# Seven block products for both matrix products of tiles 3 to 8, in 12 groups of 28 units

## The chip, the cores and the metric

The kernel runs on one core of a Trainium2 chip. The metric is the device time of one execution in microseconds (us). Engines are named as in the profile: PE (TensorE, matrix products), PEld (its weight loads), DVE (VectorE), ACT (ScalarE), POOL (GpSimd), SP (SyncE, which here issues all DMAs). SBUF is the on-chip working memory, PSUM the eight banks that TensorE accumulates in.

## The reference

Windowed attention over 8 batches of 8 heads, 576 positions of 64 values, then a two-layer network on the 4608 tokens:

```python
scores = scale * np.matmul(q, k.transpose(0, 1, 3, 2))
scores = np.where(masks[None, :, :, :], scores, -1000000000.0)
attn = softmax(scores)                 # 4 heads: the last 32 positions; 4 heads: every 4th of the last 128
x = np.matmul(attn, v)                 # brought to (4608, 512)
h = x @ w_in                           # 512 -> 2048
g = np.maximum(h, 0.0) + alpha * np.minimum(h, 0.0)
out = g @ w_out                        # 2048 -> 512
```

## The kernel before

**Precision.** Each fp32 operand of the two large products is split in a high and a low part of type fp32r, and a product is three passes: high x high, high x low, low x high (`PASSES`). A "high" is an ACT copy into fp32r, a "low" the subtraction of the high part from the value.

**Tokens.** They are cut in nine tiles of 512. Tiles 0 to 2 go through plain products in 48 *slices* (one tile, one of 16 blocks f of 128 hidden channels): `ffn_h` 12 matmuls, then the activation, then `ffn_y` 12 matmuls. The loop over n (L904 and L974) runs them one slice apart; in between it does attention for 20 pairs of heads (there are 32), the conversion of the weights, and from slice 24 on it writes the weight parts to DRAM (`save`, L442) and combines the four blocks of two neighbouring f of `w_in` into four more (`combine`, L458, on GpSimd, one 2 x 256-column set in 6 instructions; `combined_high`, L471, on ACT; `combined_low`, L476, on DVE and then two DMAs). There are 8 such sets.

**Paired stage** (`paired_stage`, L764). Tiles 3 to 8 are done in pairs (t = 3, 5, 7). For a pair, the product x @ w_in is seen as a product of 2 x 2 blocks: two tiles by two f on one side, two halves of the input channels on the other. Instead of eight block products seven are made, of combined weights and combined token blocks, whose sums give the four hidden blocks (numbered 11, 12, 21, 22: the first digit is the f, the second the tile). A block product is 6 matmuls of 128 x 128 by 512 columns (`product`, L563). `Four` (L584) is the object of one such set of four hidden blocks: `mm(q)` is block product q into bank A, B or C; `snap` an ACT copy of bank A in the middle of the sums; `add` a DVE addition of a bank and a snap; `negative` an ACT Relu(-x); `value` the DVE multiply-add that makes the activation; `high` and `low` the split into `gp`, which the second product reads. `phase_h` (L663) does four sets (28 block products), each set's vector work beside the products of the next; `phase_y` (L693) then does the second product plainly: for 4 output blocks c, 8 f and 2 tiles, 3 matmuls each, 192 in all, and 16 units of weights. There are two groups per pair. The vector work of the fourth set stands behind the first 12 matmuls of `phase_y`, and its hidden blocks are used last within each c.

**Attention** in the paired stage: 12 pairs of heads, hung on steps of `phase_y` (`attention_hooks`, L733): scores on PE, maxima on DVE, exponentials on ACT, divisions on DVE, transposes on PE, copies on ACT, values on PE, copies into the raw tokens on ACT and DVE. `token_parts` (L540) makes the seven token blocks of the next pair from raw tokens.

**Order.** Each engine executes its instructions in the order in which the program is written; nothing is reordered. Weights come from DRAM through a ring of 10 slots of 256 KB (`feed`, `take`, L513 to L520), one `feed` behind each use, on SP. PSUM has eight banks: a0 to a3 for the first product, y0 to y3 for the second.

## Time and profile before

| | |
|---|---|
| median of 3 runs | 919.82 us (919.0 to 921.11) |
| the profiled execution, its own time | 919.12 us |
| its span, first to last instruction | 917.3 us |
| mean granted TensorE clock | 0.978 |
| slices, about | up to 382.7 us |
| paired stage, three pairs of tiles | 382.7 to 574, to 749.7, to 913.2 us |

The profile's second part shows how the load is spread over the span (each digit is the busy share of one of 40 equal slices, in tenths; PEclk is the granted TensorE clock, in tenths).

```profile
PE   4668999979999998999999999999999999999998
DVE  6999487686766675676345746673347627503731
ACT  6776455453535444365445543554456306303610
POOL 0000000030222541000000000000000000000000
PEclk9879999999999998999999999999999999999999
```

Busy time counts how long instructions were in an engine; matmuls overlap each other, so their mean duration is longer than the distance from one to the next.

### The profile page before, as it was taken

Reading aid. Unit: us, or ns where it says so; the run is one execution under the profiler, and the core shown is the slowest. Engines: PE = TensorE matmul, PEld = TensorE weight load, DVE = VectorE, ACT = ScalarE, POOL = GpSimd, SP = SyncE. Lnnn points to the kernel's source line nnn. Section 1 sums busy time; section 2 is a strip of 40 time slices with the busy share of each in tenths; the row PEclk is TensorE's granted clock in tenths of the full one; section 3 lists DMA queues with packets and bytes.
Section 4 is the critical chain, followed back from the end, with each engine's and each line's share of the span. In section 5 each row is a group of like instructions: output and inputs, shape, how many; then the busy total and the mean of one; then the engine's idle time right before and its main releaser. Section 6 shows DMA issues by size and latency. Waiting matters only on the chain.

```text
span 917.3 us, 20648 instructions
## 1 busy us (share of the span) xinstructions
PE 869.6 (95%) x8080; PEld 714.5 (78%) x8080; DVE 549.4 (60%) x1607; ACT 428.1 (47%) x1250; POOL 48.8 (5%) x54
## 2 busy tenths in 40 slices
PE   4668999979999998999999999999999999999998
PEld 4556888868877886888778877887888888888886
DVE  6999487686766675676345746673347627503731
ACT  6776455453535444365445543554456306303610
POOL 0000000030222541000000000000000000000000
PEclk9879999999999998999999999999999999999999
DMA  9842152216798984475557656665466456435641
GB/s 334 295 138 70 47 189 93 91 53 202 253 305 268 305 277 152 145 209 163 174 176 200 172 179 192 201 173 155 150 165 182 145 161 195 137 103 157 183 132 46
DMA packets 101313, 159.83 MB, mean 174 GB/s; under 512 B 8416, under 2 KB 47456, under 8 KB 101216
## 3 DMA queue, kind: packets, MB, share of 16 engines
q1 hardware_dynamic: 101216, 158.51, 55.8%
q8 instruction: 64, 1.05, 0.5%
q14 instruction: 33, 0.27, 0.1%
HBM read 124.92 MB, written 33.55 MB: 173 GB/s over the span
## 4 chain that ended last, share of the span: by engine, by line
PE 87%; DVE 7%; ACT 2%; DMA 1%; issue 1%; SPq 1%; DVEq 0%; ACTq 0%
PE y L705 28%; PE pA L567 14%; PE h L375 14%; PE y L422 13%; PE pC L567 7%; PE pB L567 4%; PE o L266 3%; PE s L192 3%; PE t L248 2%; DMA ws<-w_in 1%; ACT w_dt.float L228 1%; DVE w_dt.float L216 1%; DVE w_dt.float32r L363 1%; DVE wa L352 0%; DMA w_dt.uint<-w_out 0%
## 5 line engine op out<-in xcount | busy, mean ns | idle before, releaser
L375 PE MATMUL h<-x,w_dt.float32r 128*128 128x512 f32 x576 | 150.7, 414 | 7.3 <-DVE nm L216 6.9
L422 PE MATMUL y<-g,w_dt.float32r 128*128 128x512 f32 x576 | 140.7, 393 | 0.0
L375 PEld LDWEIGHTS h<-x,w_dt.float32r 128*128 128x128 f32 x576 | 114.2, 201 | 33.0 <-issue 7.3
L422 PEld LDWEIGHTS y<-g,w_dt.float32r 128*128 128x128 f32 x576 | 106.6, 188 | 22.4 <-ACT ob L434 0.4
L705 PE MATMUL y<-gp,ring_w 128*128 128x512 f32 x480 | 113.7, 392 | 0.0
L705 PE MATMUL y<-gp,ring_xA 128*128 128x512 f32 x444 | 104.7, 391 | 1.0 <-issue 1.0
L705 PEld LDWEIGHTS y<-gp,ring_w 128*128 128x128 f32 x480 | 89.3, 188 | 18.6
L705 PEld LDWEIGHTS y<-gp,ring_xA 128*128 128x128 f32 x444 | 82.8, 188 | 18.4 <-issue 1.1
L228 ACT ACTIVATE pr<-pr,nm 128x64 f32<-128x64 f32 (+1 forms) x240 | 80.1, 335 | 28.7 <-DVE nm L216 28.7
L609 ACT COPY stage<-pA 128x512 f32<-128x512 f32 x72 | 42.3, 587 | 104.3 <-PE pA L567 104.3
L402 ACT CAST g<-m 128x512 fp32r<-128x512 f32 x48 | 29.8, 621 | 72.5 <-DVE m L397 66.2
L635 DVE TENSOR_TENSOR gp<-n,gp 128x512 fp32r<-128x512 f32 x96 | 63.2, 684 | 0.0
L627 DVE SCALAR_TENSOR_TENSOR n<-n,bal,stage 128x512 f32<-128x512 f32 x72 | 53.9, 749 | 13.9 <-ACT n L623 13.1
L567 PE MATMUL pA<-parts_w,ring_w 128*128 128x512 f32 x234 | 57.7, 390 | 0.0
L631 ACT CAST gp<-n 128x512 fp32r<-128x512 f32 x96 | 56.6, 615 | 1.9 <-DVE n L627 1.9
L567 PE MATMUL pA<-parts_w,ring_xA 128*128 128x512 f32 x228 | 56.2, 390 | 0.5 <-ACT raw_xB L302 0.5
L705 PE MATMUL y<-gp,ring_g 128*128 128x512 f32 x228 | 55.0, 393 | 0.0
L216 DVE CUSTOM_DVE_ANT_0 pr<-s,mask_sb 128x64 f32<-128x64 f32 (+1 forms) x288 | 45.0, 213 | 16.3 <-PE s L192 15.2
L623 ACT ACTIVATE n<-stage 128x512 f32<-128x512 f32 x72 | 45.6, 633 | 12.5 <-DVE stage L616 12.0
L567 PEld LDWEIGHTS pA<-parts_w,ring_w 128*128 128x128 f32 x234 | 43.8, 188 | 9.1
L728 DVE TENSOR_TENSOR ob<-y,py 128x512 f32<-128x512 f32 x24 | 16.4, 691 | 57.4 <-PE y L705 57.4
L567 PEld LDWEIGHTS pA<-parts_w,ring_xA 128*128 128x128 f32 x228 | 42.7, 188 | 9.5 <-ACT raw_xB L302 0.6
(104 smaller groups left out, 1213.5 us busy)
## 6 DMA issues: line engine op xcount, KB each, us to landing
ring_w<-wS SPq DMA_DIRECT2D x68, 256.0 KB, 2.8
ring_xA<-wS SPq DMA_DIRECT2D x67, 256.0 KB, 2.8
v<-vW SPq DMA_DIRECT2D x24, 576.0 KB, 3.9
ring_w<-wO SPq DMA_DIRECT2D x40, 256.0 KB, 2.8
ring_xA<-wO SPq DMA_DIRECT2D x37, 256.0 KB, 2.7
out<-ob SPq DMA_DIRECT2D x36, 256.0 KB, 3.2
ring_g<-wS SPq DMA_DIRECT2D x33, 256.0 KB, 2.8
wO<-w_dt.float32r SPq DMA_DIRECT2D x32, 256.0 KB, 5.2
```

The source lines that it names most:

```text
L216: nc.vector.tensor_tensor_reduce(out=self.pr[rows, r, :], in0=self.ps[e][rows, g, :], in1=mask_sb[rows, kind, :], scale=-SCALE, scalar=3.0 ...
L228: nc.scalar.activation(out=self.pr[rows, r, :], in_=self.pr[rows, r, :], func=AF.Exp, bias=self.nm[rows, r:r + 1], scale=-1.0, accum_out=s ...
L375: nc.tensor.matmul(ms[t, f], lhsT=weight(0, a, f)[:, c * P:(c + 1) * P], rhs=half(t, c)[:, e, :], start=(c == 0 and n == 0), stop=(c == NC ...
L402: nc.scalar.copy(out=g[:, 0, :], in_=ms[t, f])
L422: nc.tensor.matmul(ys[t][c], lhsT=weight(1, a, f)[:, c * P:(c + 1) * P], rhs=g[:, e, :], start=(first and n == 0), stop=(last and n == 2),)
L567: nc.tensor.matmul(to, lhsT=w[:, (2 * a + c) * P:(2 * a + c + 1) * P], rhs=part_of(name, e)[:, c * TT:(c + 1) * TT], start=start and c == ...
L609: nc.scalar.copy(out=self.s(n), in_=self.A)
L623: nc.scalar.activation(out=self.m[n], in_=self.at(n), func=AF.Relu, scale=-1.0)
L627: nc.vector.scalar_tensor_tensor(out=self.m[n], in0=self.m[n], scalar=bal[:, f:f + 1], in1=self.at(n), op0=ALU.mult, op1=ALU.add)
L631: nc.scalar.copy(out=self.g(n)[:, 0], in_=self.m[n])
L635: nc.vector.tensor_tensor(out=g[:, 1], in0=self.m.pop(n), in1=g[:, 0].bitcast(F32), op=ALU.subtract)
L705: nc.tensor.matmul(ys2[tt], lhsT=w[:, k * P:(k + 1) * P], rhs=g[:, e], start=j == 0 and n == 0, stop=j == GF - 1 and n == 2)
```

## The change

**Both products by seven.** The second product g @ w_out is now also seen as 2 x 2 blocks (two tiles by two output halves on one side, the two f of a set on the other) and made by seven block products. Of the four hidden blocks of a set, three (22, 12, 11) are split as before, and four combinations T1 to T4 of the blocks are formed (`sum`, DVE) and split too: seven splits a set where there were four. Their highs are ACT's; the low part of 22 is DVE's and the six others are GpSimd's.

**Groups of 28 units.** A group is now two sets (j = 0, 1), with four groups per pair of tiles, 12 in all. A unit is 6 matmuls and one slot of weights: units 0 to 13 are the first product's seven, alternately for j = 0 and 1; units 14 to 27 the second's seven, for output halves m = 0 and 1, each with 3 matmuls from either set. `Out.add` puts a finished bank into an SBUF result (ACT copy for three of them in a pair's first group, otherwise a DVE addition). The ring has 12 slots.

**Everything at fixed units.** `put(n, ...)` hangs an operation behind the matmuls of unit n, counted over the whole stage; `hidden` gives the places of a set's vector work, `attention` those of a pair of heads, which now come two per group in the first four groups of t = 3 and the first two of t = 5.

**Weights.** The four combinations of both matrices: 16 sets instead of 8, made in slices 23 to 27 and 31 to 41. The stores of f = 0 to 7 move to slices 8 to 15.

Core of the diff:

```diff
-GP = 4
-GF = 2 * GP
-NRING = 10
+GP = 2
+NGRP = NFP // GP
+FIRST = NFP // 2
+NRING = 12
+UNITS = 28
...
+    HORDER = (1, 7, 6, 4, 5, 2, 3)
+    YORDER = (1, 5, 6, 3, 7, 2, 4)
...
+        def sum(self, n, eng):
+            a, b = {"T1": ("21", "22"), "T2": ("11", "T1"), "T3": ("11", "21"), "T4": ("12", "T2")}[n]
...
+            eng.tensor_tensor(out=self.x[n], in0=self.m[a], in1=self.x[b] if b[0] == "T" else self.m[b], op=ALU.subtract)
...
+        TO = {1: ("A", "11", 0), 5: ("C", "22", 0), 6: ("A", "12", 0), 3: ("C", "12", 2), 7: ("A", "22", 2),
+              2: ("B", "11", 2), 4: ("A", "21", 1)}
...
+            for j in range(GP):
+                g = gblock(j, place)
+                for n, (a, e) in enumerate(PASSES):
+                    nc.tensor.matmul(
+                        self.banks[what, m], lhsT=w[:, (2 * j + a) * P:(2 * j + a + 1) * P], rhs=g[:, e],
+                        start=start and j == 0 and n == 0, stop=j + 1 == GP and n == 2, skip_group_check=True)
+            feed()
...
+            if self.grp == 0 and kind < 2:
+                nc.scalar.copy(out=to, in_=bank)
+            else:
+                nc.vector.tensor_tensor(out=to, in0=bank, in1=to, op=ALU.add)
...
+            put(n, u.scores, lambda: nxt and nxt.load_qk(), lambda: u.maxima(heads=(0,)))
+            put(n + 1, lambda: u.maxima(heads=(1,)), lambda: u.exponentials(0, 4))
+            put(n + 2, lambda: u.exponentials(4, 7))
+            put(n + 3, lambda: u.exponentials(7))
+            put(n + step - 1, u.divisions)
+            put(n + step, u.transposes, u.copies)
+            put(n + step + 2, u.values, lambda: nxt and nxt.load_v(), u.highs, u.lows)
...
+            put(n, op("snap", "s1"))
+            put(n + 2, op("snap", "s7"))
+            put(n + 4, op("snap", "s2"))
+            put(n + 6, op("add", "21"), op("negative", "21"))
+            put(n + 7, op("value", "21"))
+            put(n + 8, op("add", "22"), op("negative", "22"))
+            put(n + 9, op("value", "22"), op("sum", "T1", dve))
+            put(n + 10, op("add", "11"), op("negative", "11"), op("high", "22"), op("low", "22", dve),
+                op("high", "T1"), op("low", "T1", pool))
+            put(n + 11, op("value", "11"), op("sum", "T2", dve))
+            put(n + 12, op("negative", "12"), op("high", "T2"), op("low", "T2", pool))
+            put(n + 13, op("value", "12"), op("high", "11"), op("low", "11", pool), op("sum", "T3", dve))
+            put(n + 14, op("high", "12"), op("sum", "T4", dve))
+            put(n + 15, op("high", "T3"), op("low", "T3", pool), op("low", "12", pool))
+            put(n + 16, op("high", "T4"), op("low", "T4", pool))
...
+                for j, u in enumerate(us):
+                    hidden(n + j, u)
...
+                if t == NSTD or (todo and grp < 2):
+                    attention(n + (3 if n == 0 else 1), "y", 7)
+                    attention(n + 16, "a", 7)
+                if last and t + 2 < NTILE:
+                    ops = token_parts(t + 2)
+                    for k, names in ((2, "B11"), (3, "B11l"), (4, "T1d T3d"), (6, "T3"), (7, "T3l"), (11, "T1"), (17, "T1l"),
+                                     (18, "T2d"), (19, "T2"), (20, "T2l"), (21, "B22"), (22, "B22l"), (26, "B21"),
+                                     (27, "B21l"), (28, "T4d T4"), (29, "T4l")):
+                        put(n + k, *[ops[name] for name in names.split()])
+                for k in range(UNITS):
+                    if k < 14:
+                        us[k % 2].mm(HORDER[k // 2])
                     else:
+                        out.mm(YORDER[k // 2 - 7], k % 2)
+                    for op in at.pop(n, ()):
+                        op()
+                    n += 1
...
+    todo = [(which, i) for k in range(0, NFP, 2) for which in range(2) for i in ((k + FIRST) % NFP, (k + 1 + FIRST) % NFP)]
+    for k, n in enumerate([*range(SECOND - 1, SECOND + 4), *range(SECOND + 7, SECOND + 18)]):
+        combine_at[n] = split_at[n + 2] = *todo[k], k
...
-        if SECOND <= n < SECOND + NF:
-            save(n - SECOND)
+        if n - CUT < CUT:
+            save(n - CUT)
+        elif 0 <= n - SECOND < CUT:
+            save(n - SECOND + CUT)
```

What this makes of the order, first on DVE in the pair of tiles 7 and 8. Before: the second and third sets of `phase_h` in the last group (`pC_1_1` is bank C of group 1, set 1; `stage` holds snaps and sums, `n` values, `gp` the splits).

```order
L616 TENSOR_TENSOR stage_4750<-pC_1_1_9045,stage_4724 128x512
L627 SCALAR_TENSOR_TENSOR n_1_1_11_9082<-n_1_1_11_9082,bal,stage_4724 128x512
L627 SCALAR_TENSOR_TENSOR n_1_1_22_9094<-n_1_1_22_9094,bal,stage_4750 128x512
L627 SCALAR_TENSOR_TENSOR n_1_1_12_9105<-n_1_1_12_9105,bal,pA_1_1_9007 128x512
L616 TENSOR_TENSOR stage_4750<-pC_1_1_9045,stage_4772 128x512
L635 TENSOR_TENSOR gp_4866<-n_1_1_11_9082,gp_4866 128x512
L627 SCALAR_TENSOR_TENSOR n_1_1_21_9118<-n_1_1_21_9118,bal,stage_4750 128x512
L635 TENSOR_TENSOR gp_4866<-n_1_1_22_9094,gp_4866 128x512
L635 TENSOR_TENSOR gp_4866<-n_1_1_12_9105,gp_4866 128x512
L616 TENSOR_TENSOR stage_4772<-pB_1_2_9142,stage_4762 128x512
L635 TENSOR_TENSOR gp_4866<-n_1_1_21_9118,gp_4866 128x512
```

After: the same engine in the third group of that pair, from the value of block 22 of set 0 to the low part of block 22 of set 1 (L652, second time), which unit 14 reads. Five rows of the group (three additions, two values) stand ahead of these.

```order
L638 SCALAR_TENSOR_TENSOR stage_4800<-stage_4800,bal,stage_4798 128x512
L645 TENSOR_TENSOR stage_4798<-stage_4799,stage_4800 128x512
L624 TENSOR_TENSOR stage_4801<-pA_2_1_8071,stage_4801 128x512
L624 TENSOR_TENSOR stage_4798<-pB_2_0_8154,stage_4798 128x512
L652 TENSOR_TENSOR gp_4976<-stage_4800,gp_4976 128x512
L638 SCALAR_TENSOR_TENSOR stage_4937<-stage_4937,bal,stage_4801 128x512
L645 TENSOR_TENSOR stage_4801<-stage_4937 128x512
L638 SCALAR_TENSOR_TENSOR n_2_0_11_8163<-n_2_0_11_8163,bal,stage_4798 128x512
L645 TENSOR_TENSOR stage_4798<-n_2_0_11_8163,stage_4798 128x512
L624 TENSOR_TENSOR stage_4800<-pB_2_1_8171,stage_4800 128x512
L652 TENSOR_TENSOR gp_5007<-stage_4937,gp_5007 128x512
```

The sums (L645) are new, the low parts but one have left, and the rows of both sets alternate. The next rows of DVE, up to the first two that empty the second product's banks (L689, `yA_2_0` is bank A, output half 0, into the result `py`):

```order
L638 SCALAR_TENSOR_TENSOR n_2_0_12_8195<-n_2_0_12_8195,bal,pA_2_0_8062 128x512
L645 TENSOR_TENSOR stage_4799<-n_2_0_11_8163,stage_4799 128x512
L645 TENSOR_TENSOR stage_4799<-n_2_0_12_8195,stage_4798 128x512
L638 SCALAR_TENSOR_TENSOR n_2_1_12_8212<-n_2_1_12_8212,bal,pA_2_1_8071 128x512
L645 TENSOR_TENSOR stage_4937<-n_2_1_11_8182,stage_4937 128x512
L689 TENSOR_TENSOR py_5098<-yA_2_0_8216,py_5098 128x512
L645 TENSOR_TENSOR stage_4801<-n_2_1_12_8212,stage_4800 128x512
L689 TENSOR_TENSOR py_5098<-yA_2_1_8231,py_5098 128x512
```

So the emptying of a bank, which before came behind the whole group's vector work, stands among it. Last, ACT in the same group, from the negative of block 11 of set 0 on (L634 negatives, L648 highs):

```order
L634 ACTIVATE n_2_0_11_8163<-stage_4798 128x512
L648 CAST gp_4976<-stage_4800 128x512
L648 CAST gp_4976<-stage_4798 128x512
L634 ACTIVATE n_2_1_11_8182<-stage_4800 128x512
L648 CAST gp_5007<-stage_4937 128x512
L648 CAST gp_5010<-stage_4801 128x512
```

Ahead of both highs that a set's first splits need, ACT has the negative of block 11.

More of the change, by code (lines that the diff above doesn't have):

```diff
@@ L171, in __init__, with bank @@
             self.sm = sums[p % 2]
+            self.tags = None
+        def bank(self, side, stage, k, shape, name):
+            if self.tags is None:
+                return bank(side, shape, name)
+            return psp.tile(shape, F32, tag=self.tags[stage][k], name=name)
         def load_qk(self):
@@ L258, in values @@
         def values(self):
-            self.po = [bank("a", [P, HB, BQ], f"o_{self.id}_{u}") for u in range(2)]
+            self.po = [self.bank("a", 2, u, [P, HB, BQ], f"o_{self.id}_{u}") for u in range(2)]
             for j in range(HB):
@@ L1052, in tile_window_attention_prelu_ffn @@
             op()
-        if n >= NS - NRING + 2:
+        if n >= NS - 8 and n != NS - 4:
             feed()
     ffn_y(*slices[-1])
-    feed()
-    feed()
+    for _ in range(NRING - 7):
+        feed()
     paired_stage()
```

408 lines of the change are left out of this document (161 added, 247 removed).

## The prediction

> **What bounds the kernel now.** First the page: the busy shares and the chain that ended last.
>
> ```profile
> PE 869.6 (95%) x8080; PEld 714.5 (78%) x8080; DVE 549.4 (60%) x1607; ACT 428.1 (47%) x1250; POOL 48.8 (5%) x54
> PE 87%; DVE 7%; ACT 2%; DMA 1%; issue 1%; SPq 1%; DVEq 0%; ACTq 0%
> ```
>
> The chain is TensorE's, so time is won by fewer matmuls or lost by making TensorE wait. GpSimd (POOL) has next to no work. Next the paired stage by stretches (tiles 3 and 4, 5 and 6, 7 and 8; columns: stretch, its length, then busy time of each engine), and the chain in order of time within the last stretch, which has no attention in it.
>
> ```profile
> 382.70:574.00 191.30, 187.92 (x1914) 154.07 (x1913) 108.32 (x348) 95.95 (x291) 0.00 (x0) 1.00 0.61 186
> 574.00:749.70 175.70, 175.00 (x1317) 144.32 (x1316) 95.10 (x231) 77.29 (x195) 0.00 (x0) 1.00 0.57 165
> 749.70:913.20 163.50, 163.50 (x722) 135.11 (x720) 67.08 (x101) 51.59 (x92) 0.00 (x0) 1.00 0.48 140
> ...
> 837.05 4.08 PE pA L567 x18
> 841.13 2.72 PE pC L567 x12
> ...
> 872.41 40.81 PE y L705 x180
> ```
>
> The mean of one matmul on the page is about 390 ns, but that is its latency. In the chain twelve take 2.72 us and 180 take 40.81: a matmul costs **0.2267 us**. A pair of tiles has 720 of them, 163.2 us, which is the whole last stretch: TensorE is never late there. DVE is busy 67 of 163.5 us and ACT 52.
>
> **Matmuls removed.** A pair of tiles now takes 4 groups of 28 units of 6, so 672. 48 fewer per pair, 144 in all: 144 x 0.2267 = **32.6 us**. The stages before the paired one keep their matmuls, and attention keeps its own. The profiled execution took 919.1 us (median of the runs shown 919.8; I sum against 919.1). If nothing waits: 919.1 - 32.6 = 886.5.
>
> **Vector work that each group adds behind the first product.** A group is 28 x 1.36 = 38.1 us of TensorE, the first 14 units (19.04 us) for the hidden blocks, and unit 14 already multiplies them. Prices, with ACT and DVE rows of the last stretch for the distance from start to start:
>
> ```profile
> 838.45 0.59 ACT L609 COPY stage<-pA 128x512 f32<-128x512 f32 x1 [2.13 <-PE pA L567]
> 838.93 0.63 ACT L623 ACTIVATE n<-stage 128x512 f32<-128x512 f32 x1
> 839.07 0.69 DVE L616 TENSOR_TENSOR stage<-pC,stage 128x512 f32<-128x512 f32 x1 [1.22 <-ACT stage L609]
> 839.67 0.75 DVE L627 SCALAR_TENSOR_TENSOR n<-n,bal,stage 128x512 f32<-128x512 f32 x1
> 841.72 1.13 ACT L631 CAST gp<-n 128x512 fp32r<-128x512 f32 x2
> 844.65 1.29 DVE L635 TENSOR_TENSOR gp<-n,gp 128x512 fp32r<-128x512 f32 x2
> ...
> 254.46 2.54 POOL L466 TENSOR_TENSOR wsum_xA<-w_dt.float32r 128x512 f32<-128x512 f32 x2 [8.86 <-PE h L375]
> 257.08 3.24 POOL L469 TENSOR_TENSOR wsum_xA<-wsum_xA 128x256 f32<-128x256 f32 x4
> ```
>
> A DVE add, sum or low part lasts 0.69 and gives way after 0.60; a value lasts 0.75 and gives way after 0.67. ACT's copies, negatives and casts last 0.59 to 0.63 and give way after about 0.5. What waits for a row starts about 0.03 after its end (838.45 + 0.59 = 839.04, DVE starts 839.07). A 128x512 operation on GpSimd takes 1.27 (two in 2.54). Its low parts write fp32r where these rows write f32, which no row of GpSimd shows. On DVE that makes no difference (0.69 for one with f32, 1.29 for two with fp32r), so I take 1.27; the other end is a second run over the data for the conversion, twice 1.27 (a rival below).
>
> Before, a unit of four blocks had 11 DVE rows in 7 products; now two have 24 rows on DVE and 12 on GpSimd, and nearly all of them fall between unit 6, which completes the first block, and unit 17. What DVE and GpSimd do beside each other, from the slices where weights are combined (GpSimd's rows first, then DVE's):
>
> ```profile
> 192.66 2.98 POOL L466 TENSOR_TENSOR wsum_xB<-w_dt.float32r 128x512 f32<-128x512 f32 x2 [191.36 <-PE t L248]
> 195.72 4.18 POOL L469 TENSOR_TENSOR wsum_xB<-wsum_xB 128x256 f32<-128x256 f32 x4
> 242.35 3.25 POOL L469 TENSOR_TENSOR wsum_xB<-wsum_xB 128x256 f32<-128x256 f32 x4
> ...
> 192.97 1.52 DVE L348 TENSOR_SCALAR wa<-wa 128x512 f32<-128x512 f32 x1
> 195.84 1.21 DVE L407 TENSOR_TENSOR g<-m,g 128x512 fp32r<-128x512 f32 x1
> 196.97 1.21 DVE L352 SCALAR_TENSOR_TENSOR wa<-ws,wa 128x512 uint32<-128x512 uint32 x1
> 240.63 0.75 DVE L396 TENSOR_SCALAR m<-h,al 128x512 f32<-128x512 f32 x1 [0.98 <-PE h L375]
> 241.42 0.69 DVE L397 SCALAR_TENSOR_TENSOR m<-h,m 128x512 f32<-128x512 f32 x1
> ```
>
> While GpSimd runs, DVE rows with only SBUF inputs stretch (L407 takes 1.21 where it has 0.69 otherwise), and GpSimd's four go from 3.25 to 4.18; rows that read PSUM (L396, L397) keep their 0.75 and 0.69. So **the two take turns**, GpSimd holding about 1.0 of its 1.27. Values of 21, 22 and 11, all sums and low 22 have SBUF inputs only.
>
> The Trainium skill states this as a rule (SBUF — State Buffer, section "SBUF: two separate sides"): the port pair the two share is an exclusive lock, held for the whole instruction, against a DVE operation with two SBUF inputs. The trace agrees, except that a turn costs less than the whole GpSimd row; by the page's wording some five turns in a group would cost 0.3 us more each, about 18 us over 12 groups.
>
> Now one group without attention, each engine taking its rows in the order of the program (start-end, us from the group's start; unit k ends on TensorE at 1.36 x (k + 1), its last result 0.15 later):
>
> ```
> DVE  add21_0 9.7-10.4 | value21_0 11.1-11.9 (after neg21_0 on ACT) | add21_1 11.8 | add22_0 12.4
>      value21_1 13.2 | value22_0 13.9 | sumT1_0 14.7 | add22_1 15.3 | add11_0 15.9-16.6
> ACT  neg11_0 16.6 | high22_0 17.1-17.7 | highT1_0 17.7-18.3
> DVE  low22_0 17.8-18.5            POOL lowT1_0 18.3-19.6
> DVE  value22_1 19.6 (after POOL) | sumT1_1 20.4 | value11_0 21.0 | sumT2_0 21.8 | add11_1 22.4-23.1
> ACT  neg11_1 23.1 | high22_1 23.6-24.3
> DVE  low22_1 24.3-25.0            POOL lowT1_1 24.8-26.1, lowT2_0 26.5-27.8, low11_0, lowT2_1, low11_1 to 32.6
> DVE  value11_1 26.1 | sumT2_1 27.8 | value12_0 28.4 | sumT3_0 29.4 | sumT4_0 31.0 | value12_1 31.6
>      sumT3_1 32.6 | out(1,0) 33.2-33.9
> ```
>
> Unit 14's fifth matmul needs low22_1; without waiting it would start at 19.04 + 4 x 0.2267 = 19.95, and now at 25.0: **first wait 5.1 us**. Unit 18 adds into the bank that unit 14 filled and waits until DVE has read it, out(1,0), queued behind sum T3 of the second unit: at 33.9 where TensorE is free at 29.6, **second wait 4.4**, and 0.2 at unit 19. Group: 38.1 + 9.7 = 47.8. In a pair's first group out(1,0) is ACT's, and the walk gives 46.0 (7.9 of waiting). With two attention pairs, whose maxima, exponentials and divisions enter the same queues, the waits are 1.6 and 0.8 (transposes), 3.6 (unit 14) and 3.7 (units 18, 19): 9.7 again. Sum: 9 x 9.7 + 3 x 7.9 = **111 us**.
>
> What such a wait does to TensorE's clock:
>
> ```profile
> 200.75 1.30 PE L192 MATMUL s<-k,q 64*32 64x64 f32 x70 [4.70 <-DVE m L397]
> 201.98 4.16 PE L375 MATMUL h<-x,w_dt.float32r 128*128 128x512 f32 x12
> ...
> 349.50 2.88 PE L422 MATMUL y<-g,w_dt.float32r 128*128 128x512 f32 x12
> ...
> 434.69 1.25 PE L266 MATMUL o<-pt,v 64*64 64x32 f32 x72
> 435.87 0.98 PE L192 MATMUL s<-k,q 64*32 64x64 f32 x72
> ```
>
> Behind 4.70 of idleness twelve matmuls took 4.16 instead of the usual 2.88, 1.28 more: the clock comes back late. After the first wait that is hidden, for the second is set by DVE; after the second it is not: 1.28 for each of the nine or ten groups that have a long one, **13 us** (between 0 and 25, twice that).
>
> **The rest.** Combinations of the weights, in the slices:
>
> ```profile
> 106.00:180.00 74.00, 74.00 (x355) 60.86 (x348) 57.28 (x101) 38.12 (x71) 0.00 (x0) 1.00 0.39 128
> 286.00:352.00 66.00, 66.00 (x974) 54.57 (x972) 44.36 (x181) 33.54 (x135) 28.85 (x30) 1.00 0.86 272
> ...
> L479 DVE TENSOR_TENSOR wc<-wsum_xA,wc 128x1024 fp32r<-128x1024 f32 x6 | 7.3, 1222 | 2.8 <-ACT wc L474 2.8
> L552 DVE TENSOR_TENSOR parts_w<-raw_xB,parts_w 128x1024 fp32r<-128x1024 f32 x14 | 16.9, 1220 | 2.2 <-ACT parts_w L549 2.2
> ```
>
> Eight more of them: 5.8 us of GpSimd each (2.54 + 3.24) and 1.22 us of DVE. In this stretch of ten slices with five combinations TensorE is full while DVE is busy 44 of 66 us and GpSimd 29; five more make it 50 and 58, hidden by that slack. If it is gone, 8 x 1.22 = 10 us. The old stalls there (4.70 above) could go as well; I take 0, from -5 to +10. On SP the stores of weights 0 to 7 move to slices 8 to 15 (106 to 180 us, transfers at 0.39 of the engines' time), away from the 0.86 of the later stretch: no cost. The token blocks fall into the last groups of the first two pairs, some nine DVE rows of 1.22, 11 us each, of which up to that much can come on top of a wait. Against that, the 12 attention pairs cost 40.6 us above 163.2 now (191.3 and 175.7 us), 3.4 each, of which TensorE's own rows are about 2.6 (1.18 of o and 0.91 of s from start to start, and the transposes): some 9 us of waiting that the new waits swallow. I set these two against each other at 0, from -9 to +13. The weight ring grows to 336 units of 256 KB; at 47.8 to 53 us for 28 of them that is 140 to 155 GB/s, below the 186 that the first stretch moves now, so no wait. The end (one addition and a transfer) stays.
>
> **Sum:** 919.1 - 32.6 + 111 + 13 = **1010 us** (1010.5). Likeliest case's own range: 985 (no clock loss, shorter turns) to 1035.
>
> **Rivals.**
> *No turns between DVE and GpSimd* (say, because both mostly find the other idle). Then the walk has low22_1 at 23.8, unit 14 waits 3.8 and unit 18 only 0.6: 886.5 + 12 x 4.4 = 939, with clock losses 952. For it: GpSimd is busy only 15 of 48 us. Against: the rows at 192 to 198.
> *TensorE never waits* (the other side): 886.5. That needs DVE's sixteen rows from add21_0 to low22_1 (10.2 us at 0.60 to 0.67) packed without one hole between 9.7 and 19.95. For it: before, the same kinds of rows kept up with 163.5 us without a wait. Against: two of those rows stand behind an ACT pair that itself waits for DVE (1.2 us each), and value21_0 behind a negative (0.7). It decides from 2.7 us of waiting per group: less than 32.6 / 12 in each and the change is faster.
> *Low parts on GpSimd at 2.54 us*: GpSimd's queue then sets units 16 to 26, and the same walk has 58 us per group without attention and 67 with: 6 x 58 + 6 x 67 = 750 instead of 530.5, about 1140.
>
> **Chances.** Forecast 0.62, no turns 0.20, no waits 0.10, slow low parts 0.08. The range goes from 930 to 1035 and leaves out the last two. Faster by over 0.2% (about what a measurement of this kernel can tell from none): 0.10; within: 0.02, from cases between the first two rivals; slower: 0.88.
>
> **What would show it.** Groups of 46 to 53 us in the paired stage; TensorE idle before the second product with DVE's low part (L652) as releaser, and again four units later with DVE L689; L638 and L645 rows of 1.2 us and more beside L652 on POOL; twelve matmuls at 4 us behind the waits. I am wrong if the last stretch takes under 165 us, if SBUF-only DVE rows keep 0.69 beside GpSimd, or if the slices grow by more than 10 us.

## The result, and the profile after the change

The changed kernel takes **1023.66 us** (median of 4 runs, 1020.69 to 1025.18), the kernel before 920.47 us beside it (4 runs, 919.0 to 921.78). The ratio is **1.112, 95% interval 1.108 to 1.115**: slower. The profiled execution took 1020.69 us, its span is 1018.9 us. Of all runs in this document one, the fifth of the last kernel's six, was slow (1382.21 us at a granted clock of 0.565) and is left out of its kernel's ratio.

First the page of the changed kernel, the busy shares and the chain that ended last:

```profile
PE 887.7 (87%) x7936; PEld 705.3 (69%) x7936; DVE 717.7 (70%) x1743; ACT 480.0 (47%) x1342; POOL 336.3 (33%) x250
PE 53%; DVE 27%; ACT 9%; issue 6%; POOL 3%; DMA 2%; SPq 0%; DVEq 0%; ACTq 0%; POOLq 0%
```

TensorE has 144 matmuls fewer (7936 for 8080), and its part of the chain fell from 87% to 53%. DVE now carries 27% of it while it is busy 70% of the span: the chain runs through it without DVE being full.

Then the paired stage by pairs of tiles, as it was shown for before (stretch, length, busy time of PE, PEld, DVE, ACT, POOL, granted clock, DMA share, GB/s):

```profile
396.92:618.70 221.78, 194.61 (x1865) 150.33 (x1864) 156.11 (x388) 110.48 (x321) 77.28 (x50) 0.95 0.63 190
618.70:824.70 206.00, 180.32 (x1269) 140.40 (x1268) 143.64 (x271) 91.74 (x223) 78.31 (x50) 0.94 0.57 167
824.70:1015.00 190.30, 164.98 (x673) 130.69 (x671) 121.04 (x147) 68.30 (x121) 71.19 (x48) 0.94 0.55 159
```

The last pair, which has no attention, went from 163.5 to some 190 us, with TensorE idle in 25 of them. DVE is busy 121 of the 190, GpSimd 71: neither is full in the stage that waits.

| us, from the profiles | before | after | difference |
|---|---|---|---|
| paired stage begins (the slices' end) | 382.7 | 396.9 | +14.2 |
| paired stage, to the end of the span | 534.6 | 622.0 | +87.4 |
| span | 917.3 | 1018.9 | +101.6 |

The list of TensorE's waits (who waits, for which line, us in total, times, the longest) says where:

```profile
PE yA L678 <- ACT gp L648: 54.7, 19, 4.8
PE h L384 <- DVE nm L225: 19.2, 10, 3.5
PE t L257 <- DVE pr L247: 16.5, 12, 3.2
```

By the profile's reading the first row, which before did not have, is the second product waiting for its split blocks, 19 times. The second grew from 6.9 us in 3 waits: it belongs to the slices, where a first product (h) waits for a maximum of the attention (nm). The third, 2.2 us in 3 waits before, is the attention's transposes.

### One group, row by row

The group that starts at 870.78 is a group without attention, as the prediction walked it. TensorE (start, length, then engine, line, operation; in brackets idle time before it and its releaser):

```profile
887.10 2.88 PE L593 MATMUL pA<-parts_w,ring_w 128*128 128x512 f32 x12
889.82 0.84 PE L678 MATMUL yA<-gp,ring_w 128*128 128x512 f32 x3
894.96 4.51 PE L678 MATMUL yA<-gp,ring_w 128*128 128x512 f32 x9 [4.30 <-ACT gp L648]
899.26 3.41 PE L678 MATMUL yC<-gp,ring_xA 128*128 128x512 f32 x12
904.85 3.30 PE L678 MATMUL yA<-gp,ring_xA 128*128 128x512 f32 x12 [2.17 <-ACT gp L648]
```

DVE in the same stretch:

```profile
888.56 0.69 DVE L652 TENSOR_TENSOR gp<-stage,gp 128x512 fp32r<-128x512 f32 x1 [1.21 <-ACT gp L648]
889.17 1.85 DVE L638 SCALAR_TENSOR_TENSOR stage<-stage,bal,stage 128x512 f32<-128x512 f32 x1
...
894.93 0.69 DVE L652 TENSOR_TENSOR gp<-stage,gp 128x512 fp32r<-128x512 f32 x1 [1.20 <-ACT gp L648]
...
903.05 1.10 DVE L645 TENSOR_TENSOR stage<-n,stage 128x512 f32<-128x512 f32 x1
904.07 0.68 DVE L689 TENSOR_TENSOR py<-yA,py 128x512 f32<-128x512 f32 x1
904.67 1.16 DVE L645 TENSOR_TENSOR stage<-n,stage 128x512 f32<-128x512 f32 x1
```

And GpSimd:

```profile
889.18 1.29 POOL L652 TENSOR_TENSOR gp<-stage,gp 128x512 fp32r<-128x512 f32 x1 [23.35 <-ACT gp L648]
...
898.48 1.73 POOL L652 TENSOR_TENSOR gp<-n,gp 128x512 fp32r<-128x512 f32 x1
900.17 1.75 POOL L652 TENSOR_TENSOR gp<-stage,gp 128x512 fp32r<-128x512 f32 x1
901.88 1.72 POOL L652 TENSOR_TENSOR gp<-n,gp 128x512 fp32r<-128x512 f32 x1
```

The two chains of the prediction are there. Block 22's low part of set 0 at 888.56 (the walk: 870.78 + 17.8 = 888.58), the value behind it held up by GpSimd's row (1.85 for 0.75), the low part of set 1 at 894.93 (walk 895.08), the emptying of bank A at 904.07 (walk 903.98). TensorE stands 4.30 us at unit 14, until ACT's high of block 22 (set 1) lets its fourth matmul start; the fifth, which reads the low part, starts at 895.68 (walk 25.0 us behind the group's start, measured 24.90). It stands 2.17 us at unit 18, which starts 34.07 us behind the group's start (walk 33.9). The second wait is shorter than the 4.4 of the prediction because the matmuls ahead of it are slower: from 893.45 to 900.27 the granted clock is 0.50, and the nine of the row at 894.96 take 4.51 us, 0.5 of them the fifth's own wait. So time that was expected in the second wait stands in matmuls. The sum is what was expected: the period of the last three whole groups is 48.1 us twice and 46.1 for a pair's first, where the walk had 47.8 (and 1.28 of clock) and 46.0.

The bracket of the second wait names ACT's high (L648). The one that unit 18 reads (T2 of set 1) had been made 5 us before; what ends 0.1 us ahead of 904.85 and has to do with unit 18 is DVE's L689, which empties the bank. Whether that reading is right is tried below.

### The profile page after: what moved, and what is told of

Its sections match the earlier page's. It is cut to its first block, busy times and chain, and to the rows that moved or that the text cites. A ratio compares the mean times of both kernels' runs of the same rounds, so it can differ in the third digit from the quotient of the medians.

```text
span 1018.9 us, 21283 instructions
## 1 busy us (share of the span) xinstructions
PE 887.7 (87%) x7936; PEld 705.3 (69%) x7936; DVE 717.7 (70%) x1743; ACT 480.0 (47%) x1342; POOL 336.3 (33%) x250
## 4 chain that ended last, share of the span: by engine, by line
PE 53%; DVE 27%; ACT 9%; issue 6%; POOL 3%; DMA 2%; SPq 0%; DVEq 0%; ACTq 0%; POOLq 0%
PE h L384 12%; PE y L431 10%; PE yA L678 8%; PE pA L593 7%; PE pC L593 5%; DVE stage L645 4%; DVE n L638 4%; DVE stage L638 4%; PE yB L678 3%; DVE stage L624 3%; PE yC L678 3%; ACT gp L648 2%; PE o L275 2%; ACT stage L634 2%; PE t L257 1%
## 5 line engine op out<-in xcount | busy, mean ns | idle before, releaser
L652 POOL TENSOR_TENSOR gp<-stage,gp 128x512 fp32r<-128x512 f32 x96 | 143.0, 1499 | 380.2 <-ACT gp L648 357.5
L384 PEld LDWEIGHTS h<-x,w_dt.float32r 128*128 128x128 f32 x576 | 117.8, 208 | 46.7 <-issue 19.4
L645 DVE TENSOR_TENSOR stage<-n,stage 128x512 f32<-128x512 f32 x72 | 88.5, 1245 | 0.8
L648 ACT CAST gp<-stage 128x512 fp32r<-128x512 f32 x120 | 70.2, 613 | 26.1 <-DVE stage L645 25.8
L652 POOL TENSOR_TENSOR gp<-n,gp 128x512 fp32r<-128x512 f32 x48 | 78.1, 1626 | 0.0
L678 PE MATMUL yA<-gp,ring_w 128*128 128x512 f32 x192 | 57.4, 445 | 19.4 <-ACT gp L648 17.1
L678 PE MATMUL yA<-gp,ring_xA 128*128 128x512 f32 x192 | 56.5, 438 | 20.1 <-ACT gp L648 18.3
L689 DVE TENSOR_TENSOR py<-yA,py 128x512 f32<-128x512 f32 x78 | 53.0, 684 | 20.3 <-PE yA L678 20.1
L678 PE MATMUL yA<-gp,gp 128*128 128x512 f32 x144 | 46.3, 451 | 22.2 <-ACT gp L648 19.4
L225 DVE CUSTOM_DVE_ANT_0 pr<-s,mask_sb 128x64 f32<-128x64 f32 (+1 forms) x288 | 45.1, 211 | 26.8 <-PE s L200 25.9
L678 PEld LDWEIGHTS yA<-gp,ring_w 128*128 128x128 f32 x192 | 39.5, 212 | 34.1 <-ACT gp L648 19.5
L678 PEld LDWEIGHTS yA<-gp,ring_xA 128*128 128x128 f32 x192 | 38.5, 207 | 34.7 <-ACT gp L648 21.3
L634 ACT ACTIVATE stage<-stage 128x512 f32<-128x512 f32 x48 | 30.1, 632 | 57.8 <-DVE stage L624 57.5
```

Of the source, the lines that this page charges most:

```text
L384: nc.tensor.matmul(ms[t, f], lhsT=weight(0, a, f)[:, c * P:(c + 1) * P], rhs=half(t, c)[:, e, :], start=(c == 0 and n == 0), stop=(c == NC ...
L634: nc.scalar.activation(out=self.m[n], in_=self.at(n), func=AF.Relu, scale=-1.0)
L645: eng.tensor_tensor(out=self.x[n], in0=self.m[a], in1=self.x[b] if b[0] == "T" else self.m[b], op=ALU.subtract)
L648: nc.scalar.copy(out=self.g(n)[:, 0], in_=self.x[n] if n[0] == "T" else self.m[n])
L652: eng.tensor_tensor(out=g[:, 1], in0=self.x[n] if n[0] == "T" else self.m[n], in1=g[:, 0].bitcast(F32), op=ALU.subtract)
L678: nc.tensor.matmul(self.banks[what, m], lhsT=w[:, (2 * j + a) * P:(2 * j + a + 1) * P], rhs=g[:, e], start=start and j == 0 and n == 0, st ...
```

## The experiments

Times of single runs are compared by their profiles' stages: "slices" is the start of the paired stage, "stage" from there to the end of the span. A period is the time from a group's first matmul to the next group's.

| run | median us (runs) | slices | stage | periods with attention | plain periods |
|---|---|---|---|---|---|
| before | 920.47 (4) | 382.7 | 534.6 | | |
| the change | 1023.66 (4) | 396.9 | 622.0 | 52.7 to 55.1 | 46.1, 48.1 |
| low parts of GpSimd left out | 972.92 (1) | 393.6 | 577.5 | 49.2 to 51.1 | 43.5 to 44.5 |
| maxima first | 1017.81 (4) | 392.8 | 622.1 | as the change | as the change |
| banks emptied first | 1014.09 (1) | 398.3 | 614.0 | 52.7 to 53.0 | 46.1, 46.7 |
| low parts on DVE | 1033.03 (1) | 401.7 | 629.6 | 52.2 to 55.5 | 44.8, 48.7 |
| places spread | 931.29 (4) | 399.2 | 533.5 | 44.3, 46.3 | 39.8 to 40.0 |
| spread, low parts left out | 917.46 (1) | 398.5 | 516.6 | 44.4, 47.9 | 38.4 to 38.6 |
| spread, maxima first | 926.25 (4) | 390.4 | 532.0 | 44.3, 46.4 | 39.9, 40.0 |
| the same, saves earlier | 923.86 (9) | 387.7 | 531.9 | 44.3, 46.4 | 39.8 to 40.2 |
| other places, 10 low parts of GpSimd | 912.91 (4) | 391.4 | 519.5 | 44.4, 44.5 | 38.9 to 39.2 |
| the same, saves earlier | 909.17 (6) | 388.6 | 522.1 | 44.4, 44.5 | 38.9 to 39.2 |

("10 low parts" is per group of two sets; the change has 12. The columns of periods leave out the groups with token blocks in them and the first one of the stage.)

### Low parts of GpSimd left out

In place of each low part GpSimd writes zeros, so that the products with these low parts are left out:

```diff
         def low(self, n, eng):
             g = self.g(n)
+            if eng is nc.gpsimd:
+                eng.memset(g[:, 1].bitcast(F32), 0.0)
+                return
```

> The change, but the six low parts per set on GpSimd are replaced by a memset to zero of the same places: the low parts of these hidden blocks are left out of the output. GpSimd then reads nothing from SBUF and is quick. My theory (DVE and GpSimd take turns where both read SBUF): sums L645 fall from 1.245 us to about 0.69 each, the second wait of a group goes, the first stays at some 3.8 us because it comes from the order of DVE and ACT rows; groups of 43 us without and 50 with attention, about 60 us less than the change, 960 to 970 us. Rival (no turns; DVE rows are long for another reason, or GpSimd's own latency makes the waits): L645 stays above 1.1 us, or both waits of a group go and groups fall to 38 to 39 us.

972.92 us, a little above the 960 to 970 that were expected, and 44.5 us off the stage. The rows of the sums on DVE and GpSimd's memsets in this run (line, engine, operation, shapes and count; then busy us and mean ns):

```profile
L645 DVE TENSOR_TENSOR stage<-n,stage 128x512 f32<-128x512 f32 x72 | 48.1, 685 | 0.8
L653 POOL MEMSET gp<- 128x512 f32 x144 | 71.4, 528 | 370.5 <-PE yC L681 260.4
```

With the change they were:

```profile
L645 DVE TENSOR_TENSOR stage<-n,stage 128x512 f32<-128x512 f32 x72 | 88.5, 1245 | 0.8
```

A sum goes from 1245 to 685 ns when GpSimd writes without reading. The turns that the prediction read from the slices are real, and with them half of the stage's loss goes. (The memset also makes GpSimd's rows shorter, 0.53 us for 1.50, so the run takes out two things at once; but by the profile TensorE waited for a row of GpSimd only once in the change, 1.0 us.) Half stays: groups of 44.4 us against 38.1 of matmuls.

### Low parts on DVE

The same places, but no GpSimd in the group:

```diff
-            dve, pool = nc.vector, nc.gpsimd
+            dve, pool = nc.vector, nc.vector
```

> The change with all low parts on DVE at the same places, GpSimd idle in the paired stage. Theory (turns): on GpSimd each low part costs DVE nearly as much in blocked rows as doing it itself, so the time stays within 10 us of the change, 1015 to 1033 us, with L645 at 0.69 us and DVE busier by twelve rows a group. Rival (GpSimd takes this work off DVE): 12 x 12 x 0.6 = 86 us more, near 1100 us.

1033.03 us, at the upper end of what was expected, a stage of 629.6: 7.6 us more than the change. The sums last 686 ns, no turn is taken, and the groups are as long as ever. So neither GpSimd's slower rows nor the turns are needed for the loss: the same rows at the same places in DVE's own queue cost as much.

### Banks emptied first

The places are kept, but within a unit the addition out of a bank (L689) is written ahead of the other vector rows:

```diff
-                for j, u in enumerate(us):
-                    hidden(n + j, u)
                 for k, q in enumerate(YORDER):
                     for m in range(2):
                         put(n + 14 + 2 * k + m, lambda q=q, m=m, out=out: out.add(q, m))
+                for j, u in enumerate(us):
+                    hidden(n + j, u)
```

> The change with the emptying of the second product's banks (L689) put ahead of the other vector rows of the same unit. Theory: the second wait of a group (2.2 to 2.5 us) is the wait for DVE's L689 that is queued behind sum T3 of set 1, though the trace names ACT's cast; each L689 moves one to two rows forward, 1 to 3 us less in each group, 15 to 20 us in all, about 1005 us; the first wait stays at 4.3. Rival (the second wait is for the splits of T2, as the releaser in the trace says): nothing changes, 1020 to 1025 us.

1014.09 us, 8.0 us off the stage, about half of what was expected; a plain group goes from 48.1 to 46.7. In these groups nothing was changed for ACT (only a pair's first group empties banks there, and it stays at 46.1), so the wait at unit 18 was DVE's L689 and not the high that the trace names. The list of waits agrees: what it puts down to ACT's high falls from 54.7 us in 19 waits to 39.2 in 11, and 8 waits, 6.6 us, now stand under DVE's L689. The move is worth only 1.4 us a group; the first wait, which this leaves as it is, sets the rest.

### Places spread

If the order of the rows is the cause, another order of the same rows must take the loss away with every engine's work and all turns left in. Each row got a place of its own, so that what unit 14 reads comes first, emptied banks come between sums, and GpSimd's rows are spread from unit 14 to 24. An extract (the number is the unit; rows with the same whole number are ordered by the fraction):

```diff
-            put(n + 9, op("value", "22"), op("sum", "T1", dve))
-            put(n + 10, op("add", "11"), op("negative", "11"), op("high", "22"), op("low", "22", dve),
-                op("high", "T1"), op("low", "T1", pool))
...
+            put(n + 9.2, op("value", "22"))
+            put(n + 9.8, op("high", "22"))
+            put(n + 9.9, op("sum", "T1", dve))
+            put(n + 10, op("add", "11"))
+            put(n + 10.4, op("negative", "11"))
+            put(n + 10.4, op("low", "22", dve))
...
+            put(n + 14.2, op("low", "T1", pool))
...
+            put(n + 22.4, op("sum", "T4", dve))
+            put(n + 24.5, op("low", "T4", pool))
...
-                        put(n + 14 + 2 * k + m, lambda q=q, m=m, out=out: out.add(q, m))
+                        put(n + {1: 14.7, 5: 16.5, 6: 18.6, 3: 20.1, 7: 25.4, 2: 28.9, 4: 29.3}[q] + m, lambda q=q, m=m, out=out: out.add(q, m))
```

> The paired stage's instructions stay as they are in number, kind and engine (24 low parts of four GpSimd rows' length each per product are still on GpSimd, the same sums on VectorE, the same 336 units of matmuls). Only the places move: each vector row of a group gets a place of its own instead of up to six in one unit, the low parts of GpSimd are spread over units 14 to 24, the additions into the outputs stand between the sums, and the attention's steps are spread likewise. Theory, that the waits come from the order in which the vector rows stand on their engines: a walk along the rows with this trace's durations leaves 39 to 40 us for a group without attention and 43.5 to 44 for one with it, so the stage takes about 500 to 515 us instead of 622, and the kernel takes 900 to 915 us, less than before the change. Rival one, that GpSimd's rows and their turns with VectorE are too long for a group whatever the order: groups stay at 45 us or above, the stage at 570 or above, the kernel at 970 or more. Rival two, that the longer wait of a group is TensorE's clock and not its waits: the yA waits vanish from the list of waits and the groups stay above 44.

931.29 us (928.47 to 934.99), ratio to before 1.012 (1.009 to 1.015), a stage of 533.5 us for 622.0. Above the 900 to 915 us that were expected, 500 to 515 of it the stage, but far under the first rival's 970, and the plain groups of 39.9 are under the second's 44. The pairs of tiles:

```profile
399.20:590.70 191.50, 183.91 (x1866) 147.94 (x1865) 137.08 (x383) 110.82 (x319) 74.60 (x50) 0.97 0.71 217
590.70:769.40 178.70, 170.17 (x1275) 135.63 (x1270) 135.60 (x278) 94.46 (x226) 76.80 (x50) 0.99 0.68 200
769.40:930.00 160.60, 156.91 (x673) 124.52 (x671) 112.04 (x147) 70.53 (x121) 72.93 (x48) 1.00 0.64 184
```

The same 673 matmul rows, 147 of DVE, 121 of ACT and 48 of GpSimd as in the change's last pair, and 30 us less; the granted clock is back at 1.00. The waits of yA in the last pair went from 24.0 us for ACT gp (7 times) to this:

```profile
PE yA L678 <- DVE gp L652: 2.2, 4, 0.6
```

The turns are all still there:

```profile
L652 POOL TENSOR_TENSOR gp<-stage,gp 128x512 fp32r<-128x512 f32 x96 | 145.5, 1534 | 313.1 <-ACT gp L648 185.1
L645 DVE TENSOR_TENSOR stage<-n,stage 128x512 f32<-128x512 f32 x72 | 81.9, 1161 | 0.0
```

Sums of 1161 ns (1245 in the change) and low parts of 1534 on GpSimd (1499), in groups of 39.9 us. So 88.5 us of the stage were the order. Of what is left over the walk's 500 to 515, some 16 us stand in the two groups with token blocks, 52.0 and 48.1 us beside 44.3 and 39.9, whose rows for these blocks kept their units; 6.5 more are the stage's first group, 50.8 beside 44.3.

### Spread places, low parts of GpSimd left out

The same memset as above in the kernel with spread places; the products of GpSimd's low parts are left out again.

> The first run of the call before (places spread, all else as the change) with GpSimd's low parts filled with zeros by a memset instead of computed: their products are left out of the result. In the change's own order the same replacement shortened the paired stage by 44.6 us. Theory, that the turns between GpSimd and VectorE cost time only where the order puts a row that TensorE waits for behind them: with the places spread the replacement brings the plain groups from 39.9 us to 39 or a little above, and the paired stage from 533.5 us to 520 to 530, 4 to 13 us less. Rival, that the turns cost the same in any order: 35 us or more less.

The sums fall to 682 ns, as they did in the change's order, and the stage by 16.9 us (533.5 to 516.6) where it had been 44.5. That is a little over the 4 to 13 of the theory and under half of the rival's 35. A plain group gains 1.4 us (to 38.5, below the 39 that were expected), three of the groups with attention nothing (44.3 and 44.4), and 7.6 us of the 16.9 are one group with token blocks (48.1 to 40.5). **A turn stretches the rows of the two engines about as much in either order; what it costs the kernel depends on whether a row that TensorE is about to need stands behind it.**

### Maxima first, and spread places with them

In a slice with both, the change has the low part of the combined weights (`combined_low`, L498) ahead of the attention's maxima on DVE:

```diff
+        if scored:
+            scored.maxima()
         if n in split_at:
             combined_low(*split_at[n])
         if scored:
-            scored.maxima()
             scored.exponentials(0, 5)
```

> The change with one move in the slices: the subtraction of a weight combination (combined_low) behind the maxima of the attention pair instead of ahead of them. Theory: the 14 us by which the paired stage starts later (396.9 instead of 382.7 us) come from slices with both, where the subtraction, which waits for ACT's cast, stands on DVE ahead of the maxima, and the maxima hold the PSUM banks that the next first product needs; so the seven waits of TensorE for the maxima go, 10 to 14 us in all, 1010 to 1014 us, the paired stage unchanged at 622 us. Rival (the sixteen combinations as such overload DVE, GpSimd and the transfers there): under 4 us less.

1017.81 us (1013.74 to 1022.71), ratio 1.108 (1.103 to 1.113): 4 to 6 us less, between the theory's 10 to 14 and the rival's under 4. What the change does there, in its trace (all engines, in order of time):

```profile
326.48 0.98 PE L200 MATMUL s<-k,q 64*32 64x64 f32 x72
326.64 1.05 ACT L494 CAST wc<-wsum_xA 128x1024 fp32r<-128x1024 f32 x1 [0.26 <-PE y L431]
327.39 1.25 PE L275 MATMUL o<-pt,v 64*64 64x32 f32 x72
327.72 1.48 DVE L498 TENSOR_TENSOR wsum_xA<-wsum_xA,wc 128x1024 f32<-128x1024 f32 x1 [1.21 <-ACT wc L494]
329.12 0.21 DVE L225 CUSTOM_DVE_ANT_0 pr<-s,mask_sb 128x64 f32<-128x64 f32 x1
...
330.20 4.57 PE L384 MATMUL h<-x,w_dt.float32r 128*128 128x512 f32 x12 [1.56 <-DVE nm L225]
```

And before, in the same part of the slices:

```profile
312.22 1.23 DVE L479 TENSOR_TENSOR wc<-wsum_xA,wc 128x1024 fp32r<-128x1024 f32 x1 [0.55 <-ACT wc L474]
...
318.00 0.22 DVE L216 CUSTOM_DVE_ANT_0 pr<-s,mask_sb 128x64 f32<-128x64 f32 x1 [1.36 <-PE s L192]
```

Scores are made in every other slice. With 8 combinations the splits had fallen into the slices between; with 16 they fall into both. DVE then idles for ACT's cast and does a 1.48 us row while the maxima wait, the scores hold their banks, and the next h cannot start: 1.56 us of waiting, and twelve matmuls in 4.57 us for 2.88 behind it. The move takes this away (TensorE's waits between 200 and 400 us, the run with the move):

```profile
PE s L200 <- DVE m L406: 8.0, 3, 4.7
PE o L275 <- issue: 3.6, 1, 3.6
PE o L275 <- ACT pt L264: 1.7, 1, 1.7
PE h L384 <- DVE nm L225: 1.5, 2, 1.2
```

For nm L225 the change had 14.0 us in 8 waits there. But other waits came up: 3.6 us of o with no releaser in the profile, and 3.3 more of s for DVE's m (4.7 before the move). The six runs with the change's slices begin the paired stage at 393.6 to 401.7 (mean 398.1), the three with the maxima first at 392.8, 390.4 and 391.4 (mean 391.5): **6.5 us** from this move.

Both edits together, the spread places and this move (the run with spread places is the one that the expectation names):

> The order of the run before this one in the list, and in the slices the attention's maxima ahead of the combination of the low parts. If the two losses have nothing to do with each other, it is 4 to 10 us under that run (by what the maxima alone gave: 4.1 us by the stage's start, 8 by the slices after 272 us), about 895 to 908 us. Rival: the slices' loss lies in transfers and not in the maxima; then it is within 3 us of that run.

926.25 us, ratio 1.007 (1.005 to 1.009), 5.0 us under the run without the move, as expected; the expected level was 18 us too low, like that of the run it stands on (16).

### Saves earlier

The o that waits at 263 to 268 us was thought to need v, which SP issues among the stores of the split weights and of the combinations. In the run with spread places and maxima first the DMA engines were full there (240 to 272 us: length, busy times, clock, DMA share, GB/s):

```profile
240.00:272.00 32.00, 27.46 (x383) 22.10 (x382) 20.21 (x72) 13.76 (x54) 26.34 (x24) 0.95 0.99 310
```

In the next run, which is that one otherwise, the stores of weight blocks 8 to 11 are moved ahead to slices 16 to 22, and those of 12 to 15 to slices 24 to 27:

```diff
-        elif 0 <= n - SECOND < CUT:
-            save(n - SECOND + CUT)
+        elif n in (16, 18, 20, 22):
+            save(CUT + (n - 16) // 2)
+        elif 0 <= n - SECOND < 4:
+            save(n - SECOND + 12)
```

> The second run of this list, and the weight blocks 8 to 11 are saved in slices 16, 18, 20 and 22 and blocks 12 to 15 in slices 24 to 27, where the change saves all eight in slices 24 to 31. Theory, that what is left of the slices' loss comes from stores that stand ahead of the loads of the attention's values: the paired stage starts 3 to 8 us earlier than in that run. Rival, that those waits are of another cause: no change beyond 2 us, or a loss where the saves now crowd slices 24 to 27.

```profile
240.00:272.00 32.00, 29.05 (x398) 23.66 (x397) 21.28 (x75) 14.04 (x54) 26.23 (x24) 1.00 0.87 279
```

The share falls from 0.99 to 0.87, the wait of o from 3.0 to 1.3 us, and the stage starts 2.7 us earlier (387.7 for 390.4). The median is 2.4 us lower, 923.86, ratio 1.004 (1.002 to 1.006): a little under the 3 to 8 of the theory, over the rival's 2. So the place of the stores has a small part in the slices' loss, though the intervals of the two ratios overlap.

It is not by the path that the theory names. In the run before the move the last v issued had landed at 258.44 us, and 66 of the 72 matmuls of o had run from 262.11 on; only the last six stood until 266.47. What ends ahead of them, in this run and in the four others with this wait (maxima first, saves earlier, and both kernels with other places), is a transfer of 16 KB on the queue that the profile calls "instruction", 1.3 to 1.5 us before they go on (265.03 here). It may be what they waited for; no run tried it. Of the slices' 14 us some 5 to 6 stay unexplained (387.7 and, in the last run, 388.6 for 382.7).

### Other places, five low parts of a set on GpSimd

The maxima first, and a second set of places, in which T1's and T2's low parts are DVE's and block 22's is GpSimd's. An extract against the run with spread places and maxima first:

```diff
-            put(n + 10.4, op("low", "22", dve))
-            put(n + 14.2, op("low", "T1", pool))
-            put(n + 15.7, op("low", "T2", pool))
+            put(n + 11.5, op("low", "22", pool))
+            put(n + 11.9, op("low", "T1", dve))
+            put(n + 14.2, op("low", "T2", dve))
```

> As the run before this one in the list, but with another set of places, and the low parts of the sums T1 and T2 on VectorE while that of block 22 goes to GpSimd (five low parts on GpSimd, as many as the change has six less one). By the theory of the order the engine of a low part matters little once the places fit: within 8 us of that run, either way. Rival: GpSimd's turns cost per row wherever they stand, then it is faster by a row less per product and tile, some 24 rows of 0.4 us, about 10 us.

912.91 us, ratio to before **0.992** (0.990 to 0.994), 13.3 us under the run with spread places and maxima first, 12.5 of them in the stage. That is outside the theory's 8 us and nearer to the rival's 10. The run has other places and fewer GpSimd rows at once, and does not say which of the two did it. A fixed price per row would show in every group, and it does not: three groups with attention gained nothing (44.3 and 44.4), the plain ones 0.6 to 1.1, and the stage's first group 4.3.

The same with the earlier saves (the diff of the section above):

> The places and engines of the third run of the call before (five low parts on GpSimd, two on VectorE, maxima first) with the saves of the fourth (weight blocks 8 to 11 saved from slice 16 on). If the saves and the order of the paired stage have nothing to do with each other, it is 2 to 4 us under the 912.9 of the third, 908 to 911 us, and so 0.9 to 1.3% under the kernel before the change. Rival: the earlier saves only move a wait; then it is within 1 us of 912.9.

**909.17 us**, median of 6 runs (907.78 to 912.38 but for the one named in the first section). Ratio to before **0.988** (0.986 to 0.990). It is 3.7 us under the run before it, within what was expected; its profiled execution (912.38) starts the stage 2.8 us earlier and spends 2.6 more in it. Its busy shares:

```profile
PE 852.3 (94%) x7936; PEld 689.1 (76%) x7936; DVE 681.4 (75%) x1767; ACT 485.6 (53%) x1342; POOL 293.9 (32%) x226
```

So the change's arithmetic can beat the kernel before by 1.2%, 114 us under the kernel in the order that was measured first. (The two moves in the slices were not tried on the kernel before.)

## Why the prediction was right, and where not

**The direction and the range held** (1010 for 1023.66, range 930 to 1035), and the mechanism was the one that was forecast: two waits in each group, at unit 14 and unit 18, set by the order and the turns on DVE. The profiled execution is 10.2 us above the sum (1020.7 for 1010.5): +14.2 from the slices, -4.0 from the paired stage. That the two have opposite signs is luck.

**The matmuls removed.** 144 fewer, as counted. With the waits nearly gone they pay: plain groups of 38.9 to 39.2 us against the 38.1 computed.

**The waits, 111 us, and the clock, 13 us.** Together with -32.6 the sum gave +91.4 for the stage; +87.4 was measured. The places were right: the walk met three rows of DVE and the starts of both units in one group within 0.2 us. The clock term was mis-sized. The prediction saw that the slow clock behind the first wait is hidden in the second, and there it is; behind the second wait it put 1.28 us, where unit 18's twelve matmuls took 3.30 us for 2.88, 0.42 more. Over the whole stage TensorE's idle time grew by 74 us (78.2 for 4.1 in the three stretches shown, length less busy time), and its busy time by 13.5 with 144 matmuls fewer, so matmuls were some 46 us slower, at a granted clock of 0.94 to 0.95. That is 120 us together for the 124 of the two terms.

**The turns.** Forecast from four rows in the slices, confirmed by the memset run (1245 to 685 ns). The Trainium skill (SBUF — State Buffer, section "SBUF: two separate sides") states the same, and that only a GpSimd operation that reads SBUF takes part: the memset run agrees, 685 ns beside GpSimd's 144 writes. By the rule's other half, a lock for the whole instruction, a GpSimd row and a sum could not take under 1.85 us together (1.25 from one GpSimd row to the next and 0.60 from one sum to the next, when the other engine is out of the way); the trace has 1.68 to 1.71 from one GpSimd row to the next with a DVE row of SBUF inputs in each turn, so a turn is cheaper than the page has it, as the prediction took it, by less than the 0.3 us that it named.

But the prediction named the turns as that which decides, and gave 939 to 952 without them. With them out it is 972.92; 10.9 of these are the slices, and the rest, 962, is still 10 above. What decided was the order: with the same turns in it the stage takes 533.5 us. The prediction had the place of each row in its walk, and could have asked which rows had no reader soon.

**The rest: the step that failed** is "five more make it 50 and 58, hidden by that slack", put at 0, from -5 to +10. The slices grew by 14.2 us, which is one of the prediction's own signs of being wrong (more than 10). The slack was a mean over ten slices; the additions fell into those slices where scores wait for the same engine, ahead of them in its queue. The price of it was the maxima's delay (14.0 us of h's waits where before had 1.8), not the 10 us of DVE work that the bound was made from. Two edits took back 6.5 us (the order) and 2.7 (the stores); the rest is open. The prediction weighed the stores that it moved, and put down none for the eight added combinations, whose transfers enter the stretch that was at 0.86.

**Token blocks and attention at 0.** The group with token blocks behind attention took 62.1 us beside 53.7, and the one in the second pair 50.1 beside 48.1. Both are within the +13 that the prediction allowed. The other groups with attention took 52.2 to 55.1, where the steps gave 38.1 + 9.7 + 2 x 2.6 = 53.0, and 54.3 with the clock.

**Rivals.** "TensorE never waits" needed a packing without a hole; the change's order is no such packing, and the other places come close to one: 909.17 where 886.5 was the bound. Its threshold, 2.7 us of waiting per group, fits: plain groups of 38.9 to 39.2 are under it, and that kernel is faster than before. "Low parts at 2.54 us" fell: a row alone takes 1.29.

## What to carry to other kernels

Walk the rows of each engine in program order for one period, with durations from the trace, before trusting a busy share: here DVE at 64% and GpSimd at 37% of the last pair made it 190 us, where its 672 matmuls need 152. When such a walk shows a wait, first try to move rows that nobody needs soon behind those that somebody does; it gave 88 us here where removing the contention altogether gave 45. Slack of a stretch says nothing of the one place in it where an addition stands in front of a row that another engine waits for.

## What the runs showed of the hardware

**The clock after short waits.** Behind waits of h of 1.24 and 1.62 us twelve matmuls took 3.00 us; behind 1.50, 1.56, 1.96 and 2.00 they took 4.47 to 4.59. So waits of the same length did both. What decides can be read from the granted clock on record: in each of the twelve traces it is 1.00 or 0.50 and changes only at the edges of equal steps of 3.41 us, whatever TensorE does just then. The outcome goes with the idle time of TensorE that lies in one such step. From 100 us on, over all traces, every step at 1.00 with more than 1.95 us of it was followed by one at 0.50, none with less than 1.38 was, and between the two both occur. The wait of 1.62 us lies across an edge, 0.40 before it and 1.22 behind; 1.48 of the 1.50 us lie in one step. The steps of both, each with the next one:

```profile
296.12:299.53 3.41, 2.19 (x10) 1.83 (x11) 2.71 (x27) 3.02 (x18) 3.17 (x4) 1.00 0.94 235
299.53:302.95 3.42, 3.42 (x17) 2.83 (x16) 2.47 (x5) 1.47 (x7) 3.22 (x4) 1.00 0.87 329
360.97:364.38 3.41, 1.93 (x144) 1.74 (x127) 2.56 (x17) 1.83 (x7) 3.41 (x2) 1.00 0.48 133
364.38:367.80 3.42, 3.39 (x8) 2.74 (x9) 1.52 (x14) 3.07 (x18) 3.07 (x5) 0.50 0.95 223
```

The second wait of the group shown above, 2.17 us, lies across an edge too (1.01 and 1.16), and the clock stayed at 1.00 behind it. A wait of the values shows the two outcomes once more; first the run with other places, where 2.84 us lie in one step, then the same with the saves earlier, where 1.47 us lie across an edge:

```profile
267.48 0.31 PE L275 MATMUL o<-pt,v 64*64 64x32 f32 x6 [2.84 <-issue]
267.72 4.61 PE L431 MATMUL y<-g,w_dt.float32r 128*128 128x512 f32 x12
```

```profile
265.86 0.31 PE L275 MATMUL o<-pt,v 64*64 64x32 f32 x6 [1.47 <-issue]
266.11 3.02 PE L431 MATMUL y<-g,w_dt.float32r 128*128 128x512 f32 x12
```

The Trainium skill (TensorE: Matmul & The Clock Gate, section "Part 1: The HAM clock gate") puts the fall of the clock behind an idle window of about 3.4 us. Here 1.5 us of idle time in a step already did it in the slices, beside the attention's small matmuls; where a step holds large matmuls alone the least was 1.65.

**A GpSimd row in turns with DVE.** Alone it takes 1.29 us and a sum 0.69; in turns the rows read 1.72 to 1.75 and 1.10 to 1.78. Alone one GpSimd row starts 1.25 us behind the other and one sum 0.60 behind the other, 1.85 together; in turns the next GpSimd row starts after 1.68 to 1.71. So some 0.15 us of the two lies side by side, and DVE fits a row that reads a bank (L689, 0.68) in between at its usual time.

**A releaser can be another.** The bracket named ACT's high for the wait at unit 18; the run that moved only DVE rows in these groups shortened it.
